# Broadcasts, sums and transposes of small tensors: from TensorE products to DMA and column tiles

## The chip, the cores and the metric

The kernel runs on one core of a Trainium2 chip. The core has TensorE (PE in the profile; matrix products of 128 x 128 stationary weights with a moving operand of up to 512 columns), VectorE (DVE), ScalarE (ACT), GpSimd (POOL) and SyncE (SP), which here only issues transfers. Matrix products land in PSUM, eight banks of 512 float32 columns on 128 partitions, and VectorE or ScalarE copies them to SBUF. The metric is the device time of one execution in microseconds; the value for a kernel is the median of its runs.

## The reference, cut to what matters

The input is x, 2048 tokens of 640 channels, bfloat16. It is normalised per token (xn), and the output is `x + A(xn) + B(xn)`.

```python
# A: linear attention, 32 heads of 20 channels
q, k, v = split(xn @ wqkv)
phi = lambda t: where(t > 0, t + 1, exp(t)) + 1e-6
pq, pk = phi(q), phi(k)
kv  = einsum("bhsd,bhse->bhde", pk, v)
z   = einsum("bhsd->bhd", pk)               # sum of pk over the 2048 tokens
num = einsum("bhqd,bhde->bhqe", pq, kv)
den = einsum("bhqd,bhd->bhq", pq, z) + 1e-6
A   = (num / den) @ wo

# B: a feed-forward block on the 8 tokens with the largest r = xn @ w_r
g = silu(x_sel @ w_gate); u = x_sel @ w_up  # 8 x 1536
y = ((g * u) @ w_down) * sigmoid(r_sel)     # 8 x 640
B = xn + scatter_add(zeros, idx, y)
```

## The kernel before

It works in two stages. First, for each of 16 tiles of 128 tokens, it normalises, projects to k, forms phi(k) (`pk`) and accumulates G = xn^T pk. Then, for each of 4 blocks of 512 tokens, it forms phi(q) transposed (`pqT`, channels on partitions), the denominators, multiplies pqT by their inverses, and multiplies by Mb, which holds kv times wo. Partition q of pqT holds the channels 5q to 5q + 4, so its head is q // 4.

The line numbers at the right are those that the profile uses. `PS[:, b, ...]` is PSUM bank b. A product whose output is `PS[32*j : 32*j + 32, ...]` uses only 32 columns of the PE array, and four such products with j = 0 to 3 can stand side by side. SyncE (`sp`) issues transfers in program order.

```python
# z: sum over tokens. Strip j of the output sums the tiles 4i + j, over all 640 channels.
def zsum(b0, b1):
    for i in range(4):
        for dst, c0, c1 in ((PS[:, b0, :], 0, 512), (PS[:, b1, 0:128], 512, 640)):
            for j in range(4):
                pe.matmul(dst[32*j : 32*j+32, :], lhsT=ones32, rhs=pk[:, 4*i+j, c0:c1],    # L254
                          start=(i == 0), stop=(i == 3))
def z_ev(b0, b1):                     # hm[32j + h, c] = 1 where channel c belongs to head h
    dve.tensor_tensor(zf[:, 0:512],   PS[:, b0, :],     hm[:, 0:512],   mult)              # L494
    dve.tensor_tensor(zf[:, 512:640], PS[:, b1, 0:128], hm[:, 512:640], mult)              # L495
    act.copy(zh[:, 0, :], zf)         # high and low bfloat16 halves
def z_lo():
    dve.tensor_tensor(zh[:, 1, :], zf, zh[:, 0, :], subtract)                              # L499
def zmask(bank):                      # channels to partitions, strips summed: 10 products
    for m in range(5):
        for k in range(2):
            pe.matmul(PS[:, bank, 32*m : 32*m+32], lhsT=by5(zh[:, k, :])[:, m, :],         # L595
                      rhs=sel32[:, 0, :], start=(k == 0), stop=(k == 1))
    dve.tensor_copy(zm, PS[:, bank, 0:160])                                                # L597

def den(tb, bank):                    # 20 products; heads land on 32 partitions per strip
    for m in range(5):
        for j in range(4):
            pe.matmul(PS[32*j : 32*j+32, bank, 0:128], lhsT=zm[:, m, :],                   # L518
                      rhs=pqT[:, m, tb*512 + 128*j : ...+128], ...)
def den_ev(tb, bank):                 # inverse as exp(-ln(den))
    act.activation(ld_, PS[:, bank, 0:128], Ln, bias=1e-6)                                 # L527
    act.activation(rd, ld_, Exp, scale=-1.0)                                               # L528
def bcast(tb, bank):                  # head h to the four partitions of its channels
    for j in range(4):
        pe.matmul(PS[:, bank, 128*j : 128*j+128], lhsT=hm4[:, j, :], rhs=rds[tb], ...)     # L535
    act.copy(Rs[tb], PS[:, bank, :])                                                       # L538
def norm(tb, h0, h1):                 # Rs has two buffers
    dve.tensor_tensor(pqT[...], pqT[...], Rs[tb][:, h0:h1, :] (for all 5 m), mult)         # L545

def y_pe(b):                          # strip j sums its own 3 of the 12 chunks of 128 of F
    for k in range(3):
        for h in range(2):
            for j in range(4):
                pe.matmul(PS[32*j : 32*j+32, b+h, 128:448], lhsT=hT[:, k, 32*j : 32*j+32], # L671
                          rhs=wd[:, 3*j+k, 320*h : 320*h+320], ...)
def y_ev(b):                          # high and low halves of the strips
    act.copy(yh[:, 0, :], ...)                                                             # L677
    dve.tensor_tensor(yh[:, 1, :], ..., subtract)                                          # L678
def ysum(b):                          # sum of the four strips
    for h in range(2):
        for k in range(2):
            pe.matmul(PS[:, b+h, 128:448], lhsT=sel32, rhs=yh[:, k, 320*h : 320*h+320])    # L684
    dve.tensor_scalar(ysb, PS[...], cols[:, 1:2], mult)      # times the gate              # L686
```

The masks are built by GpSimd at the start (`hm` on 32 partitions), and ScalarE issues three transfers that copy hm to the other three strips, after the exponentials of token tile 1 and before the copy of the transposed tile 3. `hm4` and `sel32` are made on GpSimd in the first stage.

The 8 rows of y are added in memory. Tokens below 1280 are added to the output itself, the others to `hi_d`, a copy in DRAM of the residuals of tiles 10 to 15. In each case GpSimd gathers the rows by index (L736), VectorE adds y, and GpSimd scatters them (L736). Rows out of range are skipped.

```python
def hi_copy():   sp.dma_start(hi_v, XX[:, 10:16, 1, :])                 # residuals to DRAM, 960 KB
def hi_gather(): rows(xg, hi_d, idxh)                                   # 8 rows of 640
def hi_add():
    dve.tensor_tensor(xg, xg, ysb[0:8, :], add)                         # L752
    rows(hi_d, xg, idxh, scatter=True)
def hi_load():   six loads of one tile each, back to XX
def fix_gather(): rows(og, out_lo, idxu)                                # after tile 9 is stored
def fix_add():
    dve.tensor_tensor(og, og, ysb[0:8, :], add)                         # L763
    rows(out_lo, og, idxu, scatter=True)

def out_mm(t): 10 products of 320 columns, pqT tile by Mb               # L699
def out_ev(t): dve.tensor_tensor(o, PS, XX[:, t, 1, :], add); sp.dma_start(out, o)   # L720; o has 4 buffers
```

The order of the second half (m_tiled and m_full form Mb, gu is the gate and up product, q_pe the Q products L452 with two ScalarE activations L458 and L459, q_fin the last step of phi(q) on VectorE, L508; xpx corrects the residual of a tile on ScalarE, L194):

```python
... zsum(2, 4); load wd; kv_ev; q_pe(0,4); q_fin(0,3); z_ev; z_lo; q_pe(1,0); ...
... zmask(4); q_pe(1,2); ... den(0,3); ... den_ev(0,3); gates(); route3() (gates and indices to columns)
q_pe(1,4); q_fin(1,3); q_pe(2,0); q_fin(1,4); bcast(0,3); q_pe(2,1); q_fin(2,0); norm(0,0,2)
... gu_pe; den(1,3); ... gu_act; hi_copy(); den_ev(1,3); q_pe(2,2); q_fin(2,1); norm(0,2,4); q_pe(2,3); ...
q_pe(2,4); bcast(1,3); ht_pe; fix_init; hi_gather(); ... q_pe(3,0); ... y_pe; den(2,3); y_ev; den_ev(2,3)
norm(1,0,2); q_pe(3,1); ... q_pe(3,2); ... ysum(4); hi_add(); hi_load(); xpx_cols; q_pe(3,3); ... bcast(2,3)
xpx(0); q_pe(3,4); q_fin(3,3); out 0; q_fin(3,4); xpx(1); out 1; norm(1,2,4); den(3,2); den_ev(3,2); norm(2,0,2)
xpx(2); out 2; norm(2,2,4); bcast(3,3); ...; out 3; norm(3,0,2); ...; out 4; norm(3,2,4); ...; out 5 to 15
```

Of the kernel before, what the change touches and what calls it, by code (L numbers as in the profile page):

```python
# [36 lines left out]
def kernel(  # L37
# [45 lines left out]
    hm = st([P, D], BF16, "hm")  # L83
    sel32 = st([P, 4, 32], BF16, "sel32")
# [163 lines left out]
    ZA = 512  # L248

    def zsum(b0, b1):  # L250
        for i in range(4):
            for dst, c0, c1 in ((PS[:, b0, :], 0, ZA), (PS[:, b1, 0 : D - ZA], ZA, D)):
                for j in range(4):
                    pe.matmul(dst[32 * j : 32 * j + 32, :], lhsT=ones32[:], rhs=pk[:, 4 * i + j, c0:c1],  # L254
                              start=(i == 0), stop=(i == 3), skip_group_check=True)
# [8 lines left out]
    def consts_a():  # L264

        h32 = hm[0:32, :]
        pool.memset(h32, 1.0)
        for b0, sg in ((0, 1), (DH - 1, -1)):
            pool.affine_select(
                out=h32, in_=h32, compare_op=ALU.is_ge, fill=0.0,  # L270
                base=b0, pattern=[[sg, D]], channel_multiplier=-sg * DH,
            )

    def hm_copies():
        for j in range(1, 4):
            ld(act, hm[32 * j : 32 * j + 32, :], hm[0:32, :])

# [6 lines left out]
    def consts_b():  # L284
        pool.memset(sel32[:, 0, :], 0.0)
        for j in range(4):
            pool.affine_select(
                out=sel32[:, 0, :], in_=sel32[:, 0, :], compare_op=ALU.not_equal, fill=1.0,
                base=-32 * j, pattern=[[-1, 32]], channel_multiplier=1,
            )  # L290

    def consts_c():
        for j in range(1, 4):
            pool.tensor_copy(sel32[:, j, :], sel32[:, 0, :])
        pool.memset(bm1[:], 1.0)
        band(bm1[:], 0, 8)

    late = {}

    def consts_g():  # L300
        hm4 = late["hm4"] = st([P, 4, P], BF16, "hm4", "zero")
        pool.memset(hm4[:], 0.0)
        for j in range(4):
            r = slice(32 * j, 32 * j + 32)
            pool.tensor_copy(hm4[r, j, :], hm[r, :].rearrange("p (q m) -> p m q", m=KC)[:, 0, :])
# [4 lines left out]
    pool_extra = {3: consts_b, 4: consts_c, 5: consts_d, 10: consts_g}  # L310
# [23 lines left out]
    consts_a()  # L334
# [47 lines left out]
    hm_copies()  # L382
# [107 lines left out]
    zf = st([P, D], F32, "zf", "f32a")  # L490
    zh = st([P, 2, D], BF16, "zh")

    def z_ev(b0, b1):
        dve.tensor_tensor(out=zf[:, 0:ZA], in0=PS[:, b0, :], in1=hm[:, 0:ZA], op=ALU.mult)  # L494
        dve.tensor_tensor(out=zf[:, ZA:D], in0=PS[:, b1, 0 : D - ZA], in1=hm[:, ZA:D], op=ALU.mult)  # L495
        act.copy(zh[:, 0, :], zf[:])

    def z_lo():
        dve.tensor_tensor(out=zh[:, 1, :], in0=zf[:], in1=zh[:, 0, :], op=ALU.subtract)  # L499

    zm = st([P, KC, 32], BF16, "zm")
    kv1 = st([P, NG, GC], BF16, "kv1")
    kv2 = st([P, NG, GC], BF16, "kv2")
    Mb = st([P, KC, D + 1], BF16, "Mb", "wkM")

# [6 lines left out]

    rds = {}
# [10 lines left out]
    def den_ev(tb, bank):  # L524
        ld_ = tmp.tile([P, P], F32, tag="lden", name="lden")
        rd = tmp.tile([P, P], BF16, tag="rden", name="rden")
        act.activation(ld_[:], PS[:, bank, 0:P], AF.Ln, bias=eps6[:])  # L527
        act.activation(rd[:], ld_[:], AF.Exp, scale=-1.0)  # L528
        rds[tb] = rd
# [3 lines left out]
    def bcast(tb, bank):  # L533
        for j in range(4):
            pe.matmul(PS[:, bank, j * P : (j + 1) * P], lhsT=late["hm4"][:, j, :], rhs=rds[tb][:],  # L535
                      start=True, stop=True, skip_group_check=True)
        Rs[tb] = tmp.tile([P, 4, P], BF16, tag="R", name="R", bufs=2)
        act.copy(Rs[tb][:].rearrange("p j c -> p (j c)"), PS[:, bank, :])  # L538
# [17 lines left out]
    rowsf = st([1, 2, 4, 32], F32, "rowsf")  # L556
    g8 = st([1, C], BF16, "g8")
# [4 lines left out]
    ysb = st([P, D], BF16, "ysb")  # L562
# [5 lines left out]
    def route2():  # L568
        dve.max(k8[:], krow[:])
        kb = k8[:].bitcast(I32)  # L570
        dve.tensor_scalar(out=idx8[:], in0=kb, scalar1=LOW, scalar2=LOW,
                          op0=ALU.bitwise_and, op1=ALU.bitwise_xor)
        dve.tensor_scalar(out=sg8[:], in0=kb, scalar1=31, scalar2=LOW,
                          op0=ALU.arith_shift_right, op1=ALU.bitwise_and)
        dve.tensor_tensor(out=idx8[:], in0=idx8[:], in1=sg8[:], op=ALU.bitwise_xor)
        dve.tensor_scalar(out=r8[:], in0=kb, scalar1=-65536, scalar2=None, op0=ALU.bitwise_and)
        dve.tensor_copy(rowsf[:, 0, :, 0:C], idx8[:].unsqueeze(1).to_broadcast([1, 4, C]))
        for c in range(C):
            v = pool.value_load(idx8[0:1, c : c + 1], min_val=0, max_val=S - 1)
            pool.tensor_copy(xsT[:, :, c : c + 1], xnT[:, :, bass.ds(v, 1)])  # L580
# [10 lines left out]

    def zmask(bank):
        for m in range(KC):
            for k in range(2):
                pe.matmul(PS[:, bank, m * 32 : m * 32 + 32], lhsT=by5(zh[:, k, :])[:, m, :], rhs=sel32[:, 0, :],  # L595
                          start=(k == 0), stop=(k == 1), skip_group_check=True)
        dve.tensor_copy(zm[:], PS[:, bank, 0 : KC * 32].rearrange("p (m h) -> p m h", h=32))  # L597
# [44 lines left out]
    yh = st([P, 2, D], BF16, "yh", "zh")  # L642
# [24 lines left out]
    def y_pe(b):  # L667
        for k in range(3):
            for h in range(2):
                for j in range(4):  # L670
                    pe.matmul(PS[32 * j : 32 * j + 32, b + h, P : P + HW], lhsT=hT[:, k, 32 * j : 32 * j + 32],  # L671
                              rhs=wd[:, 3 * j + k, h * HW : (h + 1) * HW],
                              start=(k == 0), stop=(k == 2), skip_group_check=True)

    def y_ev(b):
        src = PS[:, b : b + 2, P : P + HW]
        act.copy(yh[:, 0, :].rearrange("p (h c) -> p h c", h=2), src)  # L677
        dve.tensor_tensor(out=yh[:, 1, :].rearrange("p (h c) -> p h c", h=2), in0=src,  # L678
                          in1=yh[:, 0, :].rearrange("p (h c) -> p h c", h=2), op=ALU.subtract)

    def ysum(b):
        for h in range(2):
            for k in range(2):
                pe.matmul(PS[:, b + h, P : P + HW], lhsT=sel32[:].rearrange("p a b -> p (a b)"),  # L684
                          rhs=yh[:, k, h * HW : (h + 1) * HW], start=(k == 0), stop=(k == 1))
        dve.tensor_scalar(out=ysb[:].rearrange("p (h c) -> p h c", h=2), in0=PS[:, b : b + 2, P : P + HW],  # L686
                          scalar1=cols[:, 1:2], scalar2=None, op0=ALU.mult)
# [38 lines left out]
    idxu = st([C, 1], I32, "idxu")  # L726
    idxh = st([C, 1], I32, "idxh")
    og = st([C, D], BF16, "og")
    xg = st([C, D], BF16, "xg")
    hi_d = drp.tile([S - TF * P, D], BF16, name="hi_d")  # L730
    hi_v = hi_d[:].rearrange("(t p) d -> p t d", p=P)
    out_lo = out[0][0 : TF * P, :]
# [8 lines left out]
    def fix_init():  # L741
        dve.tensor_copy(idxu[:], cols[0:C, 0:1])
        dve.tensor_scalar(out=idxh[:], in0=cols[0:C, 0:1], scalar1=float(TF * P), scalar2=None, op0=ALU.subtract)
# [4 lines left out]
    def hi_gather():  # L748
        rows(xg[:], hi_d[:], idxh, S - TF * P)

    def hi_add():
        dve.tensor_tensor(out=xg[:], in0=xg[:], in1=ysb[0:C, :], op=ALU.add)  # L752
        rows(hi_d[:], xg[:], idxh, S - TF * P, scatter=True)

    def hi_load():
        for t in range(TF, T):
            ld(sp, XX[:, t, 1, :], hi_v[:, t - TF, :])

    def fix_gather():
        rows(og[:], out_lo, idxu, TF * P)  # L760

    def fix_add():
        dve.tensor_tensor(out=og[:], in0=og[:], in1=ysb[0:C, :], op=ALU.add)  # L763
        rows(out_lo, og[:], idxu, TF * P, scatter=True)
# [5 lines left out]
    dve.memset(rowsf[:], 0.0)  # L770
# [15 lines left out]
    zsum(2, 4)  # L786
    wd = st([P, F // P, D], BF16, "wd", "pkwd")
    ld(sp, wd[:], B_w_down.rearrange("(fc p) n -> p fc n", p=P))
    kv_ev(3, 6)
    q_pe(0, 4, 0)  # L790
    q_fin(0, 3)
    z_ev(2, 4)
    z_lo()
# [4 lines left out]
    m_tiled(1, 2)  # L798
    m_full(0, 6, dve)
    m_full(1, 2, act)  # L800
    q_pe(1, 1, 0)
    q_fin(1, 0)
    zmask(4)
    q_pe(1, 2, 1)
    q_fin(1, 1)
    q_pe(1, 3, 2)
    q_fin(1, 2)
# [12 lines left out]
    bcast(0, 3)  # L820
    q_pe(2, 1, 2)
    q_fin(2, 0)
    norm(0, 0, 2)
# [4 lines left out]
    gu_act(6)  # L828
    hi_copy()
# [3 lines left out]
    norm(0, 2, 4)  # L833
# [4 lines left out]
    bcast(1, 3)  # L838
# [7 lines left out]
    den(2, 3)  # L846
    y_ev(6)
    den_ev(2, 3)
    norm(1, 0, 2)
    q_pe(3, 1, 1)  # L850
    q_fin(3, 0)
    q_pe(3, 2, 2)
    q_fin(3, 1)
    ysum(4)
    hi_add()
    hi_load()
# [3 lines left out]
    bcast(2, 3)  # L860
    xpx(0)
    q_pe(3, 4, 1)
    q_fin(3, 3)

    out_one(0)
# [3 lines left out]
    norm(1, 2, 4)  # L869
    den(3, 2)  # L870
    den_ev(3, 2)
    norm(2, 0, 2)
    xpx(2)
    out_one(2)
    norm(2, 2, 4)
    bcast(3, 3)
# [3 lines left out]
    norm(3, 0, 2)  # L880
    xpx(5)
    out_one(4)
    norm(3, 2, 4)
    xpx(6)
    out_one(5)
    for t in range(7, TF):
        xpx(t)
# [6 lines left out]

# [28 lines left out]
```

## Time and profile before

| | |
|---|---|
| time, median of 3 runs | 115.79 us (115.61 to 115.87) |
| span of the profiled execution | 114.1 us |
| PE, DVE, ACT, POOL instructions | 919, 212, 179, 62 |
| data moved by DMA | 18.83 MB |
| granted TensorE clock in the profiled execution | 0.998 |

The profile is one execution, recorded by the hardware. Its parts that are used here: the busy time of each engine and its share of the span; the chain that ended last, which is followed back from the last instruction to whatever released each step, so that a part of it can shorten the run if it is removed and nothing else takes its place; groups of instructions by line; the timeline, with the idle time of an engine before an instruction and who ended it; and the transfers, with the time from issue to landing. Matmuls overlap in the array, so that the durations that the timeline gives for single matmuls add up to more than the time; the chain's pieces do not overlap. A transfer's duration in the timeline is that of its issue; the landing comes later.

### The profile page before, as it was taken

The page shows a single profiled execution, that of the slowest core. Times are in us where ns is not written, and L with a number is a line of the kernel's source. Part 1 is how long each engine was busy: PE and PEld are TensorE (multiplying, and loading weights), DVE is VectorE, ACT ScalarE, POOL GpSimd, SP SyncE. Part 2 cuts the span into 40 slices and gives each one's busy share as a digit, 9 for nine tenths or more (in the row PEclk, how much of TensorE's full clock was granted, in tenths as well). Part 3 has the DMA queues.
Part 4 walks back from the last instruction along what each step waited for, and adds up shares of the span by engine and source line. Part 5 has one row for each costly group of instructions (what it writes and reads, how often), then busy time and mean ns, then how long its engine had stood idle before and what let it go on. Part 6 is the DMA issues. An engine that isn't in the chain of part 4 may idle for free.

```text
span 114.1 us, 2607 instructions
## 1 busy us (share of the span) xinstructions
PE 107.0 (94%) x919; PEld 67.0 (59%) x919; DVE 88.0 (77%) x212; ACT 76.3 (67%) x179; POOL 27.2 (24%) x62
## 2 busy tenths in 40 slices
PE   5868999999999999999999999999999999999970
PEld 2235655666666666666575556565656677777740
DVE  2589998899999997955859496569789797966670
ACT  4058697777788888561990978999998899600010
POOL 7424322376111179100000003200313200000330
PEclk9999999999999999999999999999999999999999
DMA  2999734333258563499999991090000089253332
GB/s 71 294 368 363 183 66 81 56 63 60 58 124 111 125 157 66 72 355 341 395 405 400 336 370 41 0 340 13 0 7 0 1 238 328 76 187 140 131 121 56
DMA packets 22215, 18.83 MB, mean 165 GB/s; under 512 B 10442, under 2 KB 20922, under 8 KB 22202
## 3 DMA queue, kind: packets, MB, share of 16 engines
q1 hardware_dynamic: 21600, 18.31, 53.0%
q10 hardware_dynamic: 474, 0.33, 1.0%
q8 instruction: 7, 0.11, 0.4%
q14 instruction: 6, 0.05, 0.2%
q0 software_dynamic: 128, 0.02, 0.1%
HBM read 12.80 MB, written 3.62 MB: 144 GB/s over the span
## 4 chain that ended last, share of the span: by engine, by line
PE 87%; ACT 4%; DMA 4%; DVE 2%; issue 1%
PE PS L699 19%; PE PS L452 19%; PE PS L201 18%; PE PS L232 14%; DMA XX<-in_A_x_dram 4%; PE PS L237 3%; PE PS L623 2%; PE PS L629 2%; PE PS L648 1%; ACT xnT L177 1%; PE PS L603 1%; PE PS L518 1%; ACT ek L219 1%; PE PS L173 1%; PE PS L254 1%; ACT rk L220 1%
## 5 line engine op out<-in xcount | busy, mean ns | idle before, releaser
L201 PE MATMUL PS<-wk,xnT 128*128 128x320 bf16 (+1 forms) x160 | 24.8, 300 | 0.4 <-ACT rk L220 0.2
L452 PE MATMUL PS<-xnT,wq 128*128 128x512 bf16 x100 | 23.7, 380 | 0.0
L232 PE MATMUL PS<-pk,XX 128*128 128x512 bf16 x80 | 23.3, 379 | 0.0
L699 PE MATMUL PS<-Mb,pqT 128*128 128x320 bf16 x160 | 22.4, 299 | 0.0
L201 PEld LDWEIGHTS <-xnT 128*128 128x128 bf16 x160 | 15.3, 97 | 7.7 <-ACT xnT L177 0.8
L219 ACT ACTIVATE ek<-PS 128x320 bf16<-128x320 f32 x32 | 14.3, 448 | 7.8 <-PE PS L201 7.8
L699 PEld LDWEIGHTS <-pqT 128*128 128x128 bf16 x160 | 15.4, 97 | 6.3
L458 ACT ACTIVATE qe<-PS 128x512 bf16<-128x512 f32 x20 | 12.2, 609 | 6.6 <-PE PS L452 6.1
L452 PEld LDWEIGHTS <-wq 128*128 128x128 bf16 x100 | 11.2, 118 | 8.1 <-issue 0.3
L720 DVE TENSOR_TENSOR o<-PS,XX 128x640 bf16<-128x640 f32 x15 | 12.2, 822 | 4.8 <-PE PS L699 4.0
L152 POOL TENSOR_TENSOR s<-t,halfc 128x1 bf16<-128x1 bf16 x16 | 9.6, 597 | 23.9 <-DVE t L151 23.8
L227 DVE SCALAR_TENSOR_TENSOR pk<-ek,rk 128x640 bf16<-128x640 bf16 x16 | 13.1, 817 | 2.4 <-ACT rk L220 2.1
L508 DVE SCALAR_TENSOR_TENSOR pqT<-qe,qr 128x512 bf16<-128x512 bf16 x20 | 13.3, 679 | 1.8 <-ACT qr L459 1.8
L220 ACT ACTIVATE rk<-PS 128x320 bf16<-128x320 f32 x32 | 14.4, 451 | 0.0
L237 PE MATMUL PS<-pk,XX 128*128 128x128 bf16 x64 | 14.0, 219 | 0.0
L232 PEld LDWEIGHTS <-XX 128*128 128x128 bf16 x80 | 7.8, 98 | 8.2
L459 ACT ACTIVATE qr<-PS 128x512 bf16<-128x512 f32 x20 | 12.2, 609 | 0.0
L157 ACT ACTIVATE c<-XX,MVf 128x640 bf16<-128x640 bf16 x12 | 10.4, 866 | 0.1
L137 DVE BATCH_NORM_STATS2 stats<-XX 128x6 f32<-128x320 bf16 x16 | 7.6, 474 | 2.4 <-DMA XX<-in_A_x_dram 2.4
L194 ACT ACTIVATE XX<-XX,MR,SR 128x640 bf16<-128x640 bf16 x10 | 8.6, 918 | 0.0
L166 DVE TENSOR_SCALAR XX<-c,SR 128x640 bf16<-128x640 bf16 (+2 forms) x17 | 7.0, 420 | 1.4
L715 ACT CAST o<-PS 128x160 bf16<-128x160 f32 x1 | 0.3, 292 | 11.7 <-PE PS L703 11.7
(134 smaller groups left out, 127.9 us busy)
## 6 DMA issues: line engine op xcount, KB each, us to landing
out_dram<-o SPq DMA_DIRECT2D x15, 160.0 KB, 1.8
XX<-in_A_x_dram SPq DMA_DIRECT2D x6, 320.0 KB, 5.6
wg<-in_B_w_gate_dram SPq DMA_DIRECT2D x5, 384.0 KB, 6.5
wu<-in_B_w_up_dram SPq DMA_DIRECT2D x5, 384.0 KB, 6.9
wd<-in_B_w_down_dram SPq DMA_DIRECT2D x1, 1920.0 KB, 9.1
hi_d<-XX SPq DMA_DIRECT2D x1, 960.0 KB, 4.9
XX<-hi_d SPq DMA_DIRECT2D x6, 160.0 KB, 3.2
wk<-in_A_wqkv_dram SPq DMA_DIRECT2D x2, 400.0 KB, 4.7
```

The costliest lines, as they stand in the source:

```text
L201: pe.matmul(PS[:, b + h, 0:w], lhsT=xnT[:, kc, t * P : (t + 1) * P], rhs=wk[:, kc, h * HW : h * HW + w], start=(kc == 0), stop=(kc == KC - 1),
L219: act.activation(ek[:, sl], PS[:, b + h, 0:HW], AF.Exp)
L220: act.activation(rk[:, sl], PS[:, b + h, 0:HW], AF.Relu)
L227: dve.scalar_tensor_tensor(out=pk[:, t, :], in0=ek[:], scalar=1.0, in1=rk[:], op0=ALU.min, op1=ALU.add)
L232: pe.matmul(PS[:, a, :], lhsT=lhsT, rhs=pk[:, t, 0:512], start=(t == 0), stop=(t == T - 1),)
L237: pe.matmul(PS[:, 5, a * P : (a + 1) * P], lhsT=lhsT, rhs=pk[:, t, 512:D], start=(t == 0 and a == 0), stop=(t == T - 1), skip_group_check= ...
L452: pe.matmul(PS[:, bank, :], lhsT=by5(wq[:, kc, :])[:, m, :], rhs=xnT[:, kc, tb * TBLK : (tb + 1) * TBLK], start=(kc == 0), stop=(kc == KC ...
L458: act.activation(e, PS[:, bank, :], AF.Exp)
L459: act.activation(r, PS[:, bank, :], AF.Relu)
L508: dve.scalar_tensor_tensor(out=pqT[:, m, tb * TBLK : (tb + 1) * TBLK], in0=e, scalar=1.0, in1=r, op0=ALU.min, op1=ALU.add,)
L699: pe.matmul(PS[:, b + h, 0:HW], lhsT=pqT[:, kc, t * P : (t + 1) * P], rhs=Mb[:, kc, h * HW : (h + 1) * HW], start=(kc == 0), stop=(kc == K ...
L720: dve.tensor_tensor(out=ot[:].rearrange("p (h c) -> p h c", h=2), in0=PS[:, b : b + 2, 0:HW], in1=XX[:, t, 1, :].rearrange("p (h c) -> p h ...
```

## The change

It replaces four uses of TensorE.

1. The inverse denominators go to their 128 partitions through DRAM: one transfer writes them out by head, and four transfers read them back, each to every fourth partition.
2. The z sum gives each strip of 32 columns its own range of 160 channels, over all 16 token tiles, so that a strip holds finished sums; four transfers turn each range into a column, and one VectorE product with a small mask makes zm.
3. The w_down product is divided in the same way, by output columns and not by chunks of F, so that there is nothing left to sum. y then is 4 x 32 rows of 160, and the gathers and scatters view memory as rows of 160 and use 128 indices, with 2^20 in the places without a token, which are skipped.
4. The masks hm, hm4 and sel32 and the copies of hm are gone; bm32 (128 x 32) is made instead.

The norms are moved to later places in VectorE's order, the reload of hi_d too, in two transfers of three tiles.

```diff
-    def zsum(b0, b1):
-        (16 products of 512 and 16 of 128 columns)
+    def zsum(b):
+        for t in range(T):
+            for j in range(4):
+                pe.matmul(PS[32 * j : 32 * j + 32, b, 0:GC], lhsT=ones32[:], rhs=pk[:, t, j * GC : (j + 1) * GC],
+                          start=(t == 0), stop=(t == T - 1), skip_group_check=True)      # GC = 160
...
-    def z_ev(b0, b1): ...   def z_lo(): ...   def zmask(bank): ...
+    def z_ev(b):
+        dve.tensor_copy(zs[:], PS[:, b, 0:GC])
+        for j in range(4):
+            ld(sp, zcol[32 * j : 32 * j + 32, :], zs[32 * j : 32 * j + 1, :])
+    def z_mask():
+        dve.tensor_tensor(out=zm[:], in0=zcol[:].unsqueeze(2).to_broadcast([P, KC, H]),
+                          in1=bm32[:].unsqueeze(1).to_broadcast([P, KC, H]), op=ALU.mult)
...
     def den_ev(tb, bank):
...
-        rds[tb] = rd
+        ld(sp, rd_d[tb, :, :].rearrange("h (j c) -> j h c", j=4), rd[:])
-    def bcast(tb, bank):
-        for j in range(4):
-            pe.matmul(PS[:, bank, j * P : (j + 1) * P], lhsT=late["hm4"][:, j, :], rhs=rds[tb][:], ...)
+    def bcast(tb):
         Rs[tb] = tmp.tile([P, 4, P], BF16, tag="R", name="R", bufs=2)
-        act.copy(Rs[tb][:].rearrange("p j c -> p (j c)"), PS[:, bank, :])
+        for k in range(4):
+            ld(sp, Rs[tb][k : P : 4, :, :].rearrange("h j c -> h (j c)"), rd_d[tb, :, :])
...
     def y_pe(b):
-        (24 products of 320 columns)
+        for k in range(F // P):
+            for j in range(4):
+                pe.matmul(PS[32 * j : 32 * j + 32, b, P : P + GC], lhsT=hT[:, k % 3, 32 * (k // 3) : 32 * (k // 3) + 32],
+                          rhs=wd[:, k, j * GC : (j + 1) * GC], start=(k == 0), stop=(k == F // P - 1), ...)
     def y_ev(b):
-        (high and low halves; then ysum: 4 products of 320 columns)
+        dve.tensor_scalar(out=ysb[:], in0=PS[:, b, P : P + GC], scalar1=cols[:, 1:2], scalar2=None, op0=ALU.mult)
...
-    idxu = st([C, 1], ...)   og = st([C, D], ...)   xg = st([C, D], ...)
+    idxu = st([P, 1], ...)   og = st([P, GC], ...)   xg = st([P, GC], ...)
...
     def hi_load():
-        for t in range(TF, T):
-            ld(sp, XX[:, t, 1, :], hi_v[:, t - TF, :])
+        for t in range(TF, T, 3):
+            ld(sp, XX[:, t : t + 3, 1, :], hi_v[:, t - TF : t - TF + 3, :])
```

The new order, cut to what moves:

```python
zsum(2); kv_ev; q_pe(0,4); z_ev(2); load wd; ...
q_pe(1,1); q_fin(1,0); q_pe(1,2); q_fin(1,1); q_pe(1,3); z_mask(); q_fin(1,2); ... den(0,3); ... den_ev(0,3)
q_pe(2,1); ... gu_pe; den(1,3); ... gu_act; bcast(0); hi_copy(); den_ev(1,3); ... ht_pe; fix_init; hi_gather()
... y_pe; den(2,3); bcast(1); y_ev; den_ev(2,3); q_pe(3,1); q_fin(3,0); norm(0,0,2); q_pe(3,2); q_fin(3,1); hi_add()
q_pe(3,3); q_fin(3,2); xpx(0); norm(0,2,4); q_pe(3,4); q_fin(3,3); bcast(2); out 0; q_fin(3,4); xpx(1); out 1
norm(1,0,2); den(3,2); den_ev(3,2); norm(1,2,4); hi_load(); out 2; out 3; bcast(3); norm(2,0,2); out 4; out 5
norm(2,2,4); out 6; out 7; norm(3,0,2); out 8; out 9; norm(3,2,4); out 10 to 15
```

## The prediction

> **What bounds the kernel now.** I read the page's engine shares first, then the chain that ended last in order of time, then the timeline around each instruction that the change touches, then the times from DMA issue to landing.
>
> ```profile
> PE 107.0 (94%) x919; PEld 67.0 (59%) x919; DVE 88.0 (77%) x212; ACT 76.3 (67%) x179; POOL 27.2 (24%) x62
> PE 87%; ACT 4%; DMA 4%; DVE 2%; issue 1%
> ```
>
> TensorE is busy 94% of the span and is 87% of the chain. From 15.74 us to 110.6 us every piece of the chain that the view lists is PE, so in that stretch a microsecond of PE work removed is a microsecond gained, unless a new wait takes its place. The lines of the chain that matter (start, us on the chain, what):
>
> ```profile
> 59.93 0.46 PE PS L609 x20
> 60.39 1.09 PE PS L254 x32
> ...
> 66.20 0.38 PE PS L595 x10
> ...
> 69.43 0.28 PE PS L518 x19
> ...
> 72.54 0.22 PE PS L535 x4
> ...
> 81.29 0.93 PE PS L671 x24
> ...
> 84.78 0.54 PE PS L684 x4
> ...
> 90.43 0.46 PE PS L518 x20
> ```
>
> L254 is the z sum, L595 the mask product of z, L535 the spreading of the inverse denominators (it stands in the chain four times, at 72.54, 79.79, 86.41 and 92.36, 0.22 us each), L671 the product with w_down, L684 the y sum. L518, the denominators, shows the pace of matmuls that fill only 32 columns each: twenty of them, four side by side, in 0.28 us.
>
> The timeline (start, duration, engine, line, what; in brackets the idle time before and who ended it) shows one more piece, at the start, and two places that will matter later:
>
> ```profile
> 12.36 0.59 ACTq L101 DMA_DIRECT2D hm<-hm  x1
> ...
> 12.99 0.60 ACTq L101 DMA_DIRECT2D hm<-hm  x1
> ...
> 13.62 0.60 ACTq L101 DMA_DIRECT2D hm<-hm  x1
> ...
> 14.27 0.75 ACT L177 COPY xnT<-PS 128x384 bf16<-128x384 bf16 x2 [0.95 <-PE PS L201]
> ...
> 15.74 1.56 PE L201 MATMUL PS<-wk,xnT 128*128 128x320 bf16 x10 [0.23 <-ACT rk L220]
> ...
> 81.79 1.24 POOL L736 DMA_INDIRECT xg<-hi_d,idxh  x1 [8.62 <-DVE pqT L508]
> ...
> 105.72 0.93 POOL L736 DMA_INDIRECT og<-out_dram,idxu  x1 [16.48 <-DMA out_dram<-o]
> ...
> 108.34 0.47 DVE L763 TENSOR_TENSOR og<-og,ysb 8x640 bf16<-8x640 bf16 x1
> ...
> 109.12 0.90 POOL L736 DMA_INDIRECT out_dram<-og,idxu  x1 [2.47 <-DVE og L763]
> ```
>
> ScalarE issues the three copies of the head mask hm from 12.36 to 14.22 us, and only then copies the transposed tile. That puts its exponentials late, and PE waits 0.23 us for one of them. The indirect transfers are issued by GpSimd, and VectorE's adds behind them (at 86.62 and 108.34) stand in its program order among work that PE needs.
>
> **What the Trainium skill says.** *TensorE: Matmul & The Clock Gate*, section "Back-to-back issue gap", gives N/2.4 + 2.5 ns for a warm matmul of N columns. The trace agrees: five matmuls of 512 take 1.08 us on the chain, 216 ns each. *TensorEngine Tiling (Array Packing)*, section "Tiling Modes", says that tiles work independently, and that a change of the tiling mode drains the array. The trace fits both: 0.28 us for five rounds of four is 56 ns a round, the time of one matmul of 128 columns; and L609, which comes just after full-array products, takes 0.46 us for five rounds of 160 columns, where 5 x 0.070 would be 0.35. *DMA: Bandwidth & Descriptors*, section "Anatomy of one DMA", puts the fixed cost of a small transfer near 2 us, most of it the receipt of the write. The trace has 1.8 us from issue to landing for an output store, but 4.9 us for the 0.5 KB krow copy that is issued at 56.9 us amid the weight loads. Same page, "Two DMAs through the same engine are not ordered": a transfer that reads what another wrote has to wait for the first one's completion. So write and read back of the denominators are two such times in series, and the SyncE queue that issues both stands still between them.
>
> **The change, part by part.** On PE:
> - Spreading of the denominators goes: 4 x 0.22 = 0.88 us.
> - The mask product of z goes: 0.38 us.
> - The y sum goes: 0.54 us.
> - The z sum becomes 64 matmuls of 160 columns in place of 16 of 512 and 16 of 128. Four run side by side: before 4 x 512 + 4 x 128 = 2560 columns one after another, now 16 x 160 = 2560. At the pace of L518, 0.056 x 160/128 = 0.070 us a round, that is 1.12 us against 1.09: +0.03. There is no mode change, since L609 before it has the same tiles.
> - The y product becomes 48 of 160 in place of 24 of 320: 12 x 160 against 6 x 320 columns, the same. Both follow a full-array product. 0.
>
> Sum: -1.80 + 0.03 = -1.77 us, all of it on the chain.
>
> On ScalarE the three hm issues go, about 1.8 us of its queue. The transposes that the copy at 14.27 needs are over by about 13.5, so ScalarE comes some 0.7 us earlier to the exponentials, and the 0.23 us wait of PE goes: I take -0.22. Later it loses four copies of R (2.4 us), the zh and yh copies (0.73 + 0.70). VectorE loses 0.69 + 0.28 + 0.83 + 0.31 of z work and 0.82 of yh, and gets a 160-column copy and a masked product of 160 (about 0.33 each, as L616, 325 ns, of the same width); ysb shrinks from 0.88 to about 0.33. None of this is on the chain; it is slack against what follows.
>
> New transfers, with the place each must be ready for (PE times some 0.6 to 1.9 us earlier than now):
> - z to columns: copied out at about 61.9, four small transfers at about 0.53 us of issue (as the cols copies, 508 to 558 ns), so until 64. They stand behind the last w_up load, which lands at 65.5 (58.6 + 6.9). I expect them by 66 to 66.5. VectorE comes to its masked product at about 67.9, the first denominators on PE at 68.8. Hidden, with 1.5 us to spare. w_down is issued 2.5 us later, at about 64.4, while the queues are still full, so it lands near 71 as before; it is needed at 80.
> - Denominators of block 0: ready at 71.1, write landed by 73.5 to 75, four reads issued until 75.5 to 77, landed by 79. VectorE wants them at about 83. Hidden. Block 1 has 4 us or more. Block 2 is issued after block 0's R tile is free (about 87) and lands at 91, wanted at 92.5. Block 3 comes behind the reload of hi_d and four stores, about 97, wanted at 98, and PE needs the result at 102.6. All hidden.
> - hi_d: its copy stood at 73.09; now it stands behind the reads of block 0, at 75.5 to 77, and with its 4.9 us lands at 80.4 to 82. Now it is GpSimd's gather that waits for it, no longer the index. The gather has 128 index rows of 320 bytes in place of 8 of 1280, most of them out of range. Before, 2.4 us to landing; I allow up to 1 us more. xg then is there at 84 to 86, and VectorE comes to the add at 84.5. ScalarE's next tile correction hangs on instructions behind that add, then the last Q block's activation, then block 3's denominators on PE, which now already take 0.46 in place of 0.28 us. I give back 0.3 us here.
> - End: the gather from the output goes out when tile 9 is stored, 2 us after which VectorE adds and GpSimd scatters. With 128 rows in both, add and scatter come up to 1 us later against PE. The scatter of before lands at 109.12 + 2.3 = 111.4, the last small store at 110.92 + 1.5 = 112.4. So 1 us is free, and two slower transfers in series may use it up. I give back 0.3 us.
>
> 115.79 - 1.77 - 0.22 + 0.3 + 0.3 = 114.4.
>
> **The rivals.**
> 1. *All PE, nothing given back.* For it: the chain is pure PE, and every new transfer has over 1 us to spare except two. It gives 113.8 us, and 113.4 if VectorE's and ScalarE's slack also shortens the end. Against it: the gathers with sixteen times the index rows.
> 2. *SyncE's queue becomes the bound.* One queue issues the writes, the reads back, hi_d, and the stores, in program order, and stands still while a write lands. For it: the queue stands 2 to 4 us at each of four places, and the write of the denominators is a pattern of 4 x 32 x 128 which the DMA page ("Why a DMA increments its semaphore by 16 and not by 1") would put on four engines only; no trace here shows that. If a write took 5 us, hi_d would move to 79 and the add on VectorE to 88: 2 to 3 us lost, 116 to 117. Against it: in the stretch from 71 to 92 us the queue has little else to do, and stores have four buffers.
> 3. *Many small column tiles cost more.* At the pace of L609 (0.092 a round) the z sum would be 1.47 us and y 1.10: +0.5 us, 114.9. Against it: L609 includes the mode change, and L518 with even shorter matmuls keeps full pace.
> 4. *z late under the weight loads.* If the four column transfers took 4.9 us each as krow did, the last would land at 68.9, after the product's slot at 67.9: about 0.5 to 1 us of PE. krow went out in the middle of the loads, these at their end, so I give it a small share.
>
> **Range and chances.** Rivals 1 and 3 with the two give-backs between none and double span 113.4 to 115.4, and I take 113.5 to 115.4 for 8 in 10. 2% faster is 113.47, which needs more than the whole of rival 1; 2% slower is 118.1, which needs rival 2 at its worst with another loss. So: faster 0.13, within 0.82, slower 0.05.
>
> **What would show it.** Right, if L535, L595 and L684 have no successors on PE, the z sum takes 1.1 to 1.2 us of the chain, PE's busy time falls by about 1.8 us, PE has no 0.23 us wait near 15.7, and VectorE has no idle time over 0.5 us ended by a transfer of zcol or R. The give-backs show as VectorE idle before the add to xg, PE idle before the last denominators, and a scatter that lands last. Wrong, if the chain shows SyncE's queue or a DMA between 65 and 108 us, if norm waits for R, or if the z sum takes 1.4 us.

## The result and the profile after

| | before | after |
|---|---|---|
| median | 115.75 us (115.61 to 115.87, 4 runs) | 114.34 us (113.94 to 114.99, 4 runs) |
| ratio to before, 95% interval | | 0.9884 [0.9835, 0.9934] |
| span of the profiled execution | 114.1 us | 112.8 us |

The change saves 1.2%, with an interval from 0.7% to 1.7%. The page of the kernel after, engine shares and then the chain's shares by engine:

```profile
PE 106.2 (94%) x945; PEld 66.4 (59%) x945; DVE 84.8 (75%) x210; ACT 73.8 (65%) x173; POOL 21.5 (19%) x50
PE 72%; DVE 10%; DMA 10%; POOL 2%; issue 1%; ACT 1%; POOLq 0%; DVEq 0%
```

PE's share of the chain has fallen from 87% to 72%, though PE is still busy 94% of the span: the chain now leaves PE at two places. In the chain of the kernel after (start, us on the chain, what) these pieces answer to those shown of before:

```profile
14.77 0.39 DVE XX L165
15.18 4.50 DMA xnT<-XX
19.73 1.54 PE PS L200 x10
...
60.39 1.11 PE PS L250 x64
...
69.05 0.28 PE PS L488 x20
...
80.43 0.97 PE PS L632 x48
...
82.70 3.10 DMA xg<-hi_d,idxh
85.89 0.24 DVE xg L703
...
89.61 0.24 PE PS L488 x4
89.85 18.49 PE PS L649 x135
```

L250 is the z sum, L632 the product with w_down, L488 the denominators, L649 the product with Mb; the mask product, the spreading and the y sum have no successors. New are the transposing transfer of token tile 4 before 19.73 and the gather of xg at 82.70. The same instants in both kernels show where the time went (starts from the chain and, for out 0 and the last copy, the timeline):

| instant | before | after | gained so far |
|---|---|---|---|
| z sum starts | 60.39 | 60.39 | 0 |
| block 0's denominators start (mask product gone) | 69.43 | 69.05 | 0.38 |
| w_down product starts (two spreads gone) | 81.29 | 80.43 | 0.86 |
| out 0 starts (y sum and a third spread gone) | 87.55 | 85.94 | 1.61 |
| out 2 starts, after block 3's denominators | 90.89 | 89.85 | 1.04 |
| last VectorE copy (fourth spread gone) | 110.92 | 109.66 | 1.26 |

PE gained 1.61 us up to out 0 and gave back 0.57 at block 3's denominators: the stretch between out 1 and out 2 is 0.46 us on the chain before and 1.03 after. And up to the z sum nothing was gained, where the prediction had 0.22.

The timeline of the kernel after (start, duration, engine, line, what; in brackets the idle time before and who ended it) shows the give-back in three steps:

```profile
82.70 1.56 POOL L687 DMA_INDIRECT xg<-hi_d,idxh  x1 [10.64 <-DVE pqT L480]
...
85.89 0.24 DVE L703 TENSOR_TENSOR xg<-xg,ysb 128x160 bf16<-128x160 bf16 x1 [1.19 <-DMA xg<-hi_d,idxh]
...
89.61 0.24 PE L488 MATMUL PS<-pqT,zm 128*32 128x128 bf16 x4 [0.45 <-DVE pqT L480]
```

The gather goes out at 82.70, VectorE stands 1.19 us before its add, and some 3 us later PE stands 0.45 us for the last step of phi(q), which VectorE (L480) made later. The first line gives VectorE as the releaser, but that had been done long before; what the gather waited for is found in SyncE's queue (timeline of the kernel after, SyncE alone):

```profile
71.36 0.67 SPq L100 DMA_DIRECT2D rd_d<-rden  x1
72.14 1.26 SPq L100 DMA_DIRECT2D cols<-rowsf  x2
74.57 2.67 SPq L100 DMA_DIRECT2D R<-rd_d  x4
77.28 0.60 SPq L100 DMA_DIRECT2D hi_d<-XX  x1
```

The queue stands still from 73.4 to 74.57 until the denominators are written, issues four reads, and only then the copy hi_d at 77.28 (73.09 before). That copy takes 4.5 us to land, at about 82. The add could have gone ahead at 84.7, where VectorE was free.

### The profile page after: what moved, and what is told of

It reads as the page before. It is cut to its first block, busy times and chain, and to the rows that moved or that the text cites. A ratio compares the mean times of both kernels' runs of the same rounds, so it can differ in the third digit from the quotient of the medians.

```text
span 112.8 us, 2667 instructions
## 1 busy us (share of the span) xinstructions
PE 106.2 (94%) x945; PEld 66.4 (59%) x945; DVE 84.8 (75%) x210; ACT 73.8 (65%) x173; POOL 21.5 (19%) x50
## 4 chain that ended last, share of the span: by engine, by line
PE 72%; DVE 10%; DMA 10%; POOL 2%; issue 1%; ACT 1%; POOLq 0%; DVEq 0%
PE PS L649 17%; PE PS L422 15%; PE PS L200 15%; PE PS L231 12%; DMA xnT<-XX 4%; DMA XX<-in_A_x_dram 4%; DMA xg<-hi_d,idxh 3%; PE PS L236 3%; DVE XX L165 2%; DVE pqT L480 2%; DVE stats L136 2%; POOL s L151 2%; PE PS L586 2%; PE PS L592 2%; PE PS L610 1%
## 5 line engine op out<-in xcount | busy, mean ns | idle before, releaser
L422 PE MATMUL PS<-xnT,wq 128*128 128x512 bf16 x100 | 23.1, 380 | 0.0
L649 PE MATMUL PS<-Mb,pqT 128*128 128x320 bf16 x160 | 22.3, 299 | 0.0
L649 PEld LDWEIGHTS <-pqT 128*128 128x128 bf16 x160 | 15.5, 97 | 6.3
L480 DVE SCALAR_TENSOR_TENSOR pqT<-qe,qr 128x512 bf16<-128x512 bf16 x20 | 13.6, 682 | 4.8 <-ACT qr L429 4.6
```

The source lines that it names most:

```text
L422: pe.matmul(PS[:, bank, :], lhsT=by5(wq[:, kc, :])[:, m, :], rhs=xnT[:, kc, tb * TBLK : (tb + 1) * TBLK], start=(kc == 0), stop=(kc == KC ...
L480: dve.scalar_tensor_tensor(out=pqT[:, m, tb * TBLK : (tb + 1) * TBLK], in0=e, scalar=1.0, in1=r, op0=ALU.min, op1=ALU.add,)
L649: pe.matmul(PS[:, b + h, 0:HW], lhsT=pqT[:, kc, t * P : (t + 1) * P], rhs=Mb[:, kc, h * HW : (h + 1) * HW], start=(kc == 0), stop=(kc == K ...
```

## The experiments

The repairs below differ by a few tenths, no more than the first loads vary between executions (the first K product starts between 7.05 and 7.81 us in the fourteen profiles). So beside each ratio stands the span's core: last VectorE copy minus start of the first K product, from the profile, 103.41 us before (110.92 - 7.51) and 102.20 after (109.66 - 7.46). Ratios are to the kernel before on the same chip; its median was 115.99, 115.53, 116.32 and 116.69 us in the four groups a1 to a4, a5 to b3, c1 to c3 and c4.

| run | edit to the kernel after | median, us | ratio [95%] | core, us |
|---|---|---|---|---|
| after | none | 114.34 | 0.9884 [0.9835, 0.9934] | 102.20 |
| a1 | hi_d right behind w_down | 114.11 | 0.9826 [0.9783, 0.9869] | 101.84 |
| a2 | add to xg later | 114.38 | 0.9849 [0.9809, 0.9888] | 101.51 |
| a3 | statistics of tile 5 later | 114.02 | 0.9836 [0.9788, 0.9884] | 101.68 |
| a4 | spread on PE, places of after | 114.40 | 0.984 [0.98, 0.988] | 102.51 |
| a5 | spread on PE, places of before | 114.72 | 0.9908 [0.9877, 0.994] | 103.00 |
| b1 | 0.54 us more on PE | 114.49 | 0.9887 [0.9854, 0.992] | 102.30 |
| b2 | the same in a1 | 114.51 | 0.9894 [0.9861, 0.9928] | 102.46 |
| b3 | a1 and a3 | 113.57 | 0.9809 [0.9778, 0.9839] | 101.67 |
| c1 | hi_d in between, and a3 | 114.30 | 0.9841 [0.9794, 0.9888] | 102.00 |
| c2 | a2 and a3 | 113.94 | 0.9803 [0.9764, 0.9843] | 101.17 |
| c3 | c1 and a2 | 114.58 | 0.9847 [0.9809, 0.9885] | 102.26 |
| c4 | c1, reads of block 1 later | 114.08 | 0.9787 [0.9751, 0.9823] | 101.98 |

**a1: the copy hi_d first.**

```diff
+    hi_copy()
     den_ev(0, 3)
...
     bcast(0)
-    hi_copy()
```

> The changed kernel with the copy of the residuals to DRAM (hi_d) issued before the inverse denominators of block 0, so that SyncE doesn't stand still ahead of it. Theory (the gather of hi_d came 1.2 us too late for VectorE's add, and the last denominators on PE waited for what stands behind that add): the gather starts near 80.8 and not 82.7 us, VectorE has no idle time before the add, PE's stretch from the last tile before the last denominators to the next output tile falls from 1.03 to some 0.5 us, time 113.8 to 113.9. Rival (VectorE is late because the norms were moved behind the last Q steps): PE's stretch stays near 1.0 us, time 114.3.

Measured: 0.9826 [0.9783, 0.9869]. Timeline lines of GpSimd and PE, and below them chain lines, of a1:

```profile
72.37 0.21 POOL L550 COPY xsT<-xnT 128x5 bf16 x1 [1.45 <-issue]
...
73.61 1.00 PE L610 MATMUL PS<-wg,xsT 128*32 128x384 bf16 x20 [0.18 <-POOL xsT L550]
...
80.90 1.43 POOL L687 DMA_INDIRECT xg<-hi_d,idxh  x1 [7.35 <-DMA rd_d<-rden]
```

```profile
80.58 0.94 PE PS L632 x48
...
88.97 0.46 PE PS L488 x20
89.43 18.49 PE PS L649 x135
```

The gather goes out 1.8 us earlier, the add at 84.77 has no wait, and block 3's denominators take 0.46 us, as before the change: the give-back is gone, which the late hi_d therefore caused. The first two lines show a price. GpSimd's copies of the selected tokens, usually with gaps of 0.48 to 0.51 us, come with gaps of 0.95, 1.45 and 0.77 us while hi_d moves, and PE waits 0.18 us for the last one. From the start of the z sum to that of the gate product it is 13.61 us in a1 and 13.26 after, so 0.35 of the 0.57 us is lost again there. What is left of the core's 0.36 us, about 0.15, is a shorter wait before tile 4, which this edit does not touch (see a3).

**a2: the add later on VectorE.** The copy stays late; only the place of the add changes.

```diff
-    hi_add()
     xpx_cols(0, TF)
...
     q_fin(3, 4)
+    hi_add()
```

> The changed kernel with the add to the gathered hi_d rows moved in VectorE's order, behind the last Q step (after the last phi of block 3) and not before. Theory (the late gather delays everything behind the add): the same gain as from an earlier gather, PE's stretch around the last denominators 0.5 to 0.6 us in place of 1.03, time 113.8 to 113.9, although the gather starts at 82.7 as before. Rival (moved norms): 114.3.

Measured: 0.9849 [0.9809, 0.9888]. The gather went out as late as 83.42, and the chain of a2 still has

```profile
89.05 0.46 PE PS L488 x20
```

So the late gather cost nothing by itself: it cost PE because VectorE's program order put the add ahead of Q work. In this profile the core is shorter by 0.69 us than after, 0.57 at this place and 0.12 before tile 4.

**a3: statistics of tile 5 behind tile 4's transfer.** This is the missing 0.22 us at the start.

```diff
     ln_a(5)
-    ln_b(5)
...
     tr_dma(4)
+    ln_b(5)
```

> The changed kernel with the second half of the statistics of token tile 5 moved behind the normalising of tile 4 on VectorE, so that tile 4 goes to its transposing transfer 0.4 us sooner. Theory (the ScalarE time won at the start is lost since PE waits for the transposing transfer of tile 4): PE starts the K products of tile 4 at 19.3 and not 19.73 us and everything behind comes 0.3 to 0.4 us earlier, time 113.9 to 114.0. Rival (another limit stands right behind, the next transposes or the phi of the first tiles): the K products of tile 5 still start at 22.4 us, time 114.3.

Measured: 0.9836 [0.9788, 0.9884]. Timeline of PE, first two lines from the kernel after, then one from a3:

```profile
15.15 1.53 PE L200 MATMUL PS<-wk,xnT 128*128 128x320 bf16 x10
...
19.73 0.45 PE L200 MATMUL PS<-wk,xnT 128*128 128x320 bf16 x2 [0.44 <-DMA xnT<-XX]
```

```profile
18.95 1.53 PE L200 MATMUL PS<-wk,xnT 128*128 128x320 bf16 x10
```

After the change tile 3's product starts at 15.15 (15.74 before, with its 0.23 us wait), so the early wait is gone as predicted. But tile 4 comes to PE through the first transposing transfer, issued at 15.18 and landed 4.5 us later (2.6 us is the median of the twelve), and PE stands 0.44 us for it. With the statistics out of its way PE does not wait, and tile 4 starts 0.78 us earlier, 0.34 of it from an earlier first K product (7.12 in place of 7.46), so that the edit is worth 0.44 us. Block 3's denominators still wait 0.39 us in a3, so this is a separate gain.

The earlier issue is not what helps, though. In a3 the transfer is issued at 14.76 and lands 2.6 us later, as it did before the change (issued at 15.38, landed at 17.96; PE came to it only at 19.74). In the kernel after, 15 of the transfer's 16 completion signals are there by 17.74, long before PE needs them, and the last one comes at 19.68. The trace's single packets show a 16 KB packet of the queue that the profile lists as "q8 instruction", from 17.30 to 18.52; two of the transfer's last 32 small writes come at its end, at 18.50, the other 30 by 17.31. In a1, a2, a4, a5, b1 and b2 two writes are late in the same way, and tile 4 follows tile 3 by 4.27 to 4.44 us (4.58 after). Before, and in the six kernels with a3's edit, all 32 are out before that packet starts, and tile 4 follows by 3.97 to 4.00 us. So the transfer is late where its end meets that packet, and in a3 it ends ahead of it; that the packet holds the writes up is read from these times, and no run moves it alone.

**a4 and a5: the spread back on PE.** Both put the four products and the ScalarE copy of before in place of the transfers through DRAM. In a4 they stand where the changed kernel has its reads; since products and denominators share a PSUM bank there, the spread of one block overwrites the denominators of the next, so a4 computes with wrong denominators and its time is that of the work alone. a5 has the spreads where the kernel before had them.

```diff
-        ld(sp, rd_d[tb, :, :].rearrange("h (j c) -> j h c", j=4), rd[:])
...
-        for k in range(4):
-            ld(sp, Rs[tb][k : P : 4, :, :].rearrange("h j c -> h (j c)"), rd_d[tb, :, :])
+        for j in range(4):
+            pe.matmul(PS[:, bank, j * P : (j + 1) * P], lhsT=hm4[:, j, :], rhs=rds[tb][:], ...)
+        act.copy(Rs[tb][:].rearrange("p j c -> p (j c)"), PS[:, bank, :])
```

> One part of the change undone: the inverse denominators are spread by four PE products and a ScalarE copy per block again, everything else as changed; no transfers of rd_d and R. Theory (PE work is time, but the transfers cost the wait before the last denominators): PE gets 0.88 us more, SyncE issues hi_d at once and the wait of 0.57 us goes, time 114.6 to 114.7. Rival A (the transfers cost nothing, the wait has another cause): 115.2. Rival B (the transfers cost more than the PE work they replace, by traffic as well): under 114.3.

> As a4_pe_spread, but with the four spreads in the places where the kernel before has them, so that none overwrites denominators in the shared PSUM bank. Theory: 0.88 us of PE more than the changed kernel and no wait of 0.57 us, so the last output 0.3 to 0.5 us later, ratio to before 0.991. Rival A (the transfers cost nothing): 0.996. Rival B (the transfers cost more than the products): below 0.988.

Measured: a4 0.984 [0.98, 0.988], a5 0.9908 [0.9877, 0.994]. Timeline of a5:

```profile
80.94 1.43 POOL L700 DMA_INDIRECT xg<-hi_d,idxh  x1 [9.10 <-DVE pqT L490]
...
86.78 0.59 ACT L519 CAST R<-PS 128x512 bf16<-128x512 f32 x1 [0.47 <-DVE pqT L526]
...
89.94 0.24 PE L498 MATMUL PS<-pqT,zm 128*32 128x128 bf16 x4 [0.38 <-DVE pqT L490]
```

The gather is early again, and yet the denominators wait 0.38 us: here ScalarE's copy of R (0.59 us), which a5's chain passes through, stands ahead of the last Q activations. So this stretch has more than one way to be late, and the two arrangements can't be compared by the spread alone. Counted from the first K product, as in the table, a4 is 0.31 us longer than the kernel after, which is the 0.88 us of PE put back less the 0.57 of the give-back, as its theory said; a5 is 0.80 us longer, so that its ratio came out as expected, but not for the reason given, since most of the wait stayed. The ratios don't settle it: a4's is below that of the kernel after, a5's above, and both intervals overlap with its own. What the transfers are worth by themselves is thus known only to a few tenths.

**b1 and b2: is PE's time still the end's?** Four products of 320 columns, 0.54 us, are added ahead of the Q product at 83 us; nothing reads them. b1 has them in the kernel after, b2 in a1.

```diff
     xpx_cols(0, TF)
+    for h in range(4):
+        pe.matmul(PS[:, 4 + h % 2, 0:HW], lhsT=ident[:], rhs=wq[:, 0, 0:HW], ...)
     q_pe(3, 3, 0)
```

> The changed kernel with four extra PE products of 320 columns into an unused place, just before the last two Q steps: the PE work of the removed y sum (0.54 us) put back, with nobody waiting for it. Theory (PE is not what sets the time there, VectorE's late add is): the extra work fills the wait before the last denominators, PE's stretch there falls from 1.03 to some 0.5 us, and the time stays at that of the changed kernel within 0.1 us, ratio to before 0.988. Rival (PE sets the time throughout): 0.5 us more, ratio 0.993.

> The same four extra products in the kernel that copies the residuals first (a1_hi_first), where the wait is gone. Theory: now the extra work is paid in full, its output tiles begin 0.5 us later than in a1_hi_first, ratio to before 0.987 where a1_hi_first had 0.983. Rival (such products are hidden anyway, as they depend on nothing): the ratio of a1_hi_first.

Measured: b1 0.9887 [0.9854, 0.992] against 0.9884 for after, b2 0.9894 [0.9861, 0.9928] against 0.9826 for a1. Chain of b1, then of b2 (L807 is the added work):

```profile
85.82 0.24 DVE xg L703
...
89.54 0.24 PE PS L488 x4
89.78 18.49 PE PS L649 x135
```

```profile
80.44 0.94 PE PS L632 x48
...
83.95 0.54 PE PS L807 x4
...
89.38 0.46 PE PS L488 x20
```

In b1 the extra PE work is free once xg is there: from VectorE's add to out 2 it is 3.96 us in b1 (85.82 to 89.78) and 3.96 after (85.89 to 89.85), and PE's wait is down from 0.45 to 0.16 us. From the w_down product on b1 is 0.25 us longer all the same (9.67 against 9.42), since its gather landed that much later. In b2 the work is paid in full: from the w_down product to out 2 it is 9.40 us (80.44 to 89.84) against 8.85 in a1 (80.58 to 89.43). This shows that in the kernel after the stretch from the add to out 2 belongs to VectorE, and in a1 to PE.

**b3: a1 and a3 together.**

> The changed kernel with both repairs, the residuals copied first and the statistics of tile 5 later. Theory (two separate losses, 0.5 us before the last denominators and 0.4 to 0.6 us at tile 4): they add, PE's stretch around the last denominators 0.46 us and the K products of tile 4 from about 19.0 us, the last output near 108.2, 113.2 us, ratio to before 0.977. Rival (the second loss only uncovers the first again, or another wait): 0.982 as with each alone.

Measured: 0.9809 [0.9778, 0.9839], 113.57 us. The core is 0.53 us shorter than after: 0.45 gained before tile 4 and 0.57 at block 3's denominators, less 0.49 between z sum and gate product (13.75 us in place of 13.26), where the wait for GpSimd's copies has grown to 0.32 us. So the two gains add, and the price of the early hi_d eats nearly one of them:

```profile
73.55 1.00 PE L610 MATMUL PS<-wg,xsT 128*32 128x384 bf16 x20 [0.32 <-POOL xsT L550]
```

**c1 to c4: repairs without that wait.** c1 puts hi_d between the index columns and the reads of block 0 (and has a3); c2 is a2 with a3; c3 is c1 with a2; c4 is c1 with block 1's reads behind block 2's denominators.

```diff
c1, c3, c4:
+    hi_copy()
     bcast(0)
-    hi_copy()
c4:
-    bcast(1)
     y_ev(6)
     den_ev(2, 3)
+    bcast(1)
```

> The copy of the residuals is put between the read of the four index columns and the reads of block 0's inverse denominators (SyncE order: rd_d, cols, hi_d, R), and the statistics of tile 5 stand behind tile 4's transposing transfer as before. Theory (the copy is late only because it stands behind four dependent reads, and early copies slow GpSimd's index reads): hi_d issues near 73.4 us, PE has no wait over 0.25 us for the xsT copies, the gather goes out by 81.5, the last denominators' stretch is 0.46 us, and the time is 0.3 us under the kernel with the copy behind w_down: ratio 0.977 to 0.980. Rival (the wait for xsT is GpSimd's own, or hi_d at 73.4 delays the reads of R instead): same as that kernel, ratio 0.981 or above, with a wait over 0.25 us left.

> The add to xg moved on VectorE behind the last Q block's correction, and the statistics of tile 5 behind tile 4's transfer. Theory: both repairs add, den stretch 0.46 us with the gather still late, K product of tile 4 without wait; ratio 0.978 to 0.981. Rival (the two gains end in the same later wait and do not add): 0.983 or above.

> The two repairs of the gather (copy between the index columns and the reads of R; add later on VectorE) and the statistics together. Theory (each repair of the gather alone removes the whole wait): equal to the better of the two kernels with one of them, within 0.15 us. Rival (part of the wait is left with one repair): 0.2 us or more under both.

> The kernel with the copy of the residuals in the middle (c1) lost 0.8 us around the product with w_down and block 2's denominators: the product took 1.13 us instead of 0.94, and PE then stood 0.44 us with nothing shown that it waits for. There the four reads of block 1's inverse denominators ran during the product (from 79.58 us), which they do in no kernel without that loss. Here these reads stand behind block 2's denominators' write. Theory (the reads slow the 136 short matrix and weight instructions of that stretch): product at 0.94 to 0.97 us, denominators 0.28 us without idle time before, time 0.7 us under c1's, ratio 0.977 to 0.980. Rival (the gather on GpSimd, which starts 0.4 us into the product there too, or something else): the stall stays, ratio 0.983 to 0.985.

Measured: c1 0.9841 [0.9794, 0.9888], c2 0.9803 [0.9764, 0.9843], c3 0.9847 [0.9809, 0.9885], c4 0.9787 [0.9751, 0.9823]. c2 came out as its theory said: its core is 1.03 us shorter than after, 0.45 before tile 4 and 0.57 at block 3's denominators, without a price. In c1 hi_d went out at 72.61, the gather at 80.00, PE had no wait for xsT and 0.46 us for block 3's denominators, all as expected, and yet there was no gain over a3 (core 102.00 against 101.68). The chains of c1, c2 and c4 around the w_down product:

```profile
79.67 1.13 PE PS L632 x48
80.80 0.04 PE PS L488 x3
80.84 0.44 issue
81.28 0.44 PE PS L488 x17
```

```profile
79.87 0.94 PE PS L632 x48
80.82 0.28 PE PS L488 x20
```

```profile
79.73 1.12 PE PS L632 x48
80.85 0.03 PE PS L488 x2
80.88 0.44 issue
81.32 0.44 PE PS L488 x17
```

In c1 the same 68 short products take 2.05 us that take 1.22 in c2, with 0.44 us in which PE waits for nothing that the profile shows; in c3 it is 0.70 us, and so c3, expected within 0.15 us of the better of c1 and c2, is 0.64 us behind c2. I had put the loss down to the reads of block 1, which run during the product in c1. c4 moves them to 83.18, and the loss is there unchanged, so that theory falls. The gather starts 0.4 us into the product there, but it does so in a1 as well, without loss (80.90 against 80.51). All three kernels that stall issue hi_d at about 72.6; what connects the two stays open. c4's ratio is the lowest, yet its profile has the stall and a core 0.81 us longer than c2's, and the intervals of b3, c2 and c4 overlap: of these three none is shown to be the fastest. Their intervals reach into that of the kernel after by 0.0008 at most, so that they are probably better than it; the clearest sign is c2's core.

## Why the prediction was right, step by step

The prediction of 114.4 us was met at 114.34, and that closely by luck: of its four terms only the largest held, and the errors of the others (0.22 and 0.27 us too hopeful, 0.3 us too cautious) nearly cancel.

- **PE -1.77: right.** Mask product, spreads and y sum went by their amounts. The z sum took 1.11 us (predicted 1.12), the w_down product 0.97 where no change was predicted from 0.93. Together -1.80 + 0.02 + 0.04 = -1.74 us. PE's busy time fell only from 107.0 to 106.2, not by the 1.8 that I had named as a sign. Busy time is a sum of overlapping records, and the sign was badly chosen; the instants in the table carry this point.
- **Early wait -0.22: wrong, 0.** PE's wait at 15.74 did go, but the step took it that everything behind would move up with it. The next tile's transposing transfer did not: before it had landed 1.8 us ahead of PE, after it landed at 19.68, and PE stood 0.44 us for it. That tile 4 starts at the same instant in both (19.74 and 19.73) is chance: PE's own work led up to it before, the transfer after. a3 removes the new wait.
- **First give-back +0.3: right mechanism, mis-sized.** Gather waiting for hi_d, VectorE's add, last Q block, block 3's denominators, in that order. a1 and a2 each break the sequence at another link, and both restore 0.46 us. The term measured 0.57. The transfer was not slower than I had allowed: hi_d landed at 82 (80.4 to 82 predicted) and xg at 85.8 (84 to 86 predicted). What was mis-sized is what this lateness costs: xg came near the late end of its range, VectorE waited 1.19 us for it, and 0.57 us of that, about half, reached PE as a longer stretch (0.45 us of it shown as waiting), where I had taken 0.3.
- **Second give-back +0.3: wrong, 0.** In the timeline of the kernel after the tail's transfers keep clear of the end:

```profile
104.66 1.03 POOL L687 DMA_INDIRECT og<-out_dram,idxu  x1 [16.87 <-DMA out_dram<-o]
...
107.08 0.23 DVE L714 TENSOR_TENSOR og<-og,ysb 128x160 bf16<-128x160 bf16 x1
...
107.80 1.02 POOL L687 DMA_INDIRECT out_dram<-og,idxu  x1 [2.10 <-DVE og L714]
...
109.65 0.37 ACTq L100 DMA_DIRECT2D out_dram<-o  x1
```

  The add has no idle time, and the scatter issued at 107.80 lands 2.3 us later, at 110.1, while ScalarE's store of 109.65 lands at about 111.15, and SyncE's last one is issued at 110.01. The step failed where it let 128 index rows cost more than 8: gather and scatter of the output landed in 2.2 and 2.3 us before and in 2.3 us each after.
- **Sum.** -1.74 + 0 + 0.57 + 0 = -1.17 us against -1.26 at the last copy; 0.05 of the difference is the earlier first K product.
- **Rival 1** (all PE, nothing given back) fell by the 0.57. **Rival 2** (SyncE's queue) failed as the bound: SyncE's waits in the kernel after (us in total, times, longest) have

```profile
SPq L100 <- DMA rd_d<-rden: 6.2, 3, 3.6
```

  but R made VectorE wait only once, 0.34 us before block 3's norm at 99.63, where PE did not stop. Its standing still does explain the late hi_d. The Trainium skill, *DMA: Bandwidth & Descriptors*, "Two DMAs through the same engine are not ordered", says why the wait has to be there: the engine that issues a transfer which reads what another one wrote must wait for the first one's completion. In the trace SyncE does so for up to 3.6 us. The near 2 us that the prediction takes from "Anatomy of one DMA" stand there for transfers that GpSimd issues; here block 0's write of the denominators took 3.2 us (71.36 to 74.57) and the reads 2.2 us (median). **Rival 3** (slow column tiles) fell with the z sum's 1.11 us, **rival 4** with z's masked product, which ran at 67.97 without a wait.
- **Signs of being wrong.** Two of them came though the number held: the chain shows a DMA between 65 and 108 us, the gather at 82.70, and a norm waited for R. The first is the first give-back itself, so this sign contradicted a term of the same prediction; the second cost PE nothing.

## What to carry to other kernels

Moving work from the bounding engine to transfers pays by the engine time removed less what the in-order queues do to their neighbours: here not the new transfers were late, but an old one queued behind them. Look for the old transfer whose consumer stands early in another engine's program order, and move either of the two; a2 needed one line. Test a suspected slack with dummy work on the bounding engine: if it is free, the stretch belongs to something else. Compare intervals inside each profile for this, not instants of two profiles: the first K products alone lay up to 0.76 us apart here.

## What was not expected of the hardware

- Indirect transfers with 128 indices, at least 96 of them out of range and skipped, landed in 2.3 us (gather and scatter of the output, scatter to hi_d), and 3.1 us for the gather from hi_d; with 8 indices it was 2.2 to 2.9 us. GpSimd spent 1.02 to 1.56 us on each, where it had spent 0.90 to 1.82 us with 8 indices.
- The first transposing transfer took 4.5 us where the median of its kind is 2.6: fifteen of its sixteen completion signals were there after 2.6 us, and the sixteenth came 1.9 us later, in a transfer that ended while a 16 KB packet of the instruction queue moved.
- Small GpSimd copies with gaps of about 0.5 us (one of 0.88) came with gaps of up to 1.45 us while a 960 KB copy was moving.
- A stretch of 68 short products, 1.22 us in c2, lost 0.8 us without a shown cause in c1 and c4 and 1.1 in c3; the runs don't settle why.
